# Scaling the rows of x by their gate ahead of the transposes, in four tiles of a routed expert layer

## The chip, the cores and the metric

One core of a Trainium2 chip runs the kernel. The metric is device time in microseconds (us): the median of several executions. The profile and the trace show one further execution; its times count from the start of its span. Engines are called as the profile calls them: PE is TensorE (PEld its weight loads), DVE is VectorE, ACT is ScalarE, POOL is GpSimd, SP is SyncE, which here only issues transfers.

## The reference

```python
def reference(**kwargs):
    attn_out = _attn_ref(**attn_kwargs)          # (4, 8, 544, 64)
    x = attn_out.transpose(0, 2, 1, 3).reshape(B * S, H * D)   # 2176 rows of 512
    x = _moe_ref(x=x, **moe_kwargs)
    return _moe2_ref(x=x, **moe2_kwargs)

def _moe_ref(x, w_gate, w1, w2, capacity):
    probs = softmax(x @ w_gate)                  # 8 experts
    expert_idx = np.argmax(logits, axis=1)
    gate_w = probs[np.arange(N), expert_idx]
    ...
    h = np.maximum(np.einsum('ecd,edf->ecf', disp, w1), 0.0)
    y = np.einsum('ecf,efd->ecd', h, w2)
    out[i] = gate_w[i] * y[expert_idx[i], pos[i]]

def _moe2_ref(x, w_in, w_out):
    h = x @ w_in
    g = h * np.clip(h + 3.0, 0.0, 6.0) / 6.0
    return g @ w_out
```

A row goes to one expert. Its gate is a positive number, and the expert is linear but for a ReLU, so that gate times expert(x) and expert(gate times x) are the same up to rounding.

## The kernel before

Three phases follow each other. The first computes the attention, the routing and the lists of rows of each expert, and one tile of the expert layer. The second, the loop of this case (`for s in range(N0, NF)`, s from 1 to 5), runs five tiles of 256 rows through their experts; "loop tile s" is one of them. The third multiplies all rows by the two last weight matrices, 16 slices of the inner size one after the other; its first group, of two row tiles, still converts the 64-bit words of these matrices to float (`vconv`, three DVE operations a piece, L1147, L1149, L1151), and `advance` spreads this conversion over the loop and that group.

The order of the work on each engine is that of the code: every engine takes its instructions in program order, and a wait holds all that stand behind it. One loop tile does this, in this order:

- `m1` (matmuls L904): four quarters q of the hidden layer, `xT` times W1, 24 matmuls each, in an exact split into high and low parts. Each quarter is taken out of PSUM by ACT (`ht` high part, `hth`, L908) and then by DVE (low part, `htl`, L910).
- After quarter 0 (`after0`): where the tile begins a new expert, the split of W2 (`split`, L825 on ACT, L827 with three pieces on DVE and one on POOL); then the gate row: PE transposes the 256 gates, broadcast to 128 columns, into PSUM (`row_turn`, L890, names `pgb`), and ACT copies them to `gB` (L894). After quarter 1 (`after1`): one `vconv` on DVE.
- `xt` (L847, `pxt`): PE transposes the gathered rows `xg` of the next tile, eight transposes; ACT and DVE take out high and low part (L850, L852).
- In tiles 2 and 4 transposes of a second stream, the half tiles (`p_...`), and in tiles 1 and 3 the split of W1 for the next expert.
- `m2` (L922): two halves of 48 matmuls. After the first half is taken out (`y_part`, L932: DVE multiplies PSUM, which holds y transposed, by the gate row and writes `y`), `between` computes the gate of the next tile (`gate`, L865 to L879: seven small DVE operations and one exponential on ACT). `y_out` sends y to DRAM.

`pm` in the rows stands for the PSUM tiles of `m1` and `m2`; four of them are in turn. The lines that matter for the gate:

```python
        hT = m1(xT.pop(s), {0: after0, 1: after1})
        ...
            xT[s + 1] = xt(xg[s + 1])
        ...
        m2(hT, ids.pop(s), gBs.pop(s), slice(256 * s, 256 * s + 256), between)
```

## Time and profile before

| | |
|---|---|
| median of 3 runs | 544.25 us (543.48 to 544.5) |
| the profiled execution | 542.06 us, of it 540.3 us span |
| granted TensorE clock, mean | 0.997 |
| PE busy | 524.3 us (97%) |
| DVE busy | 300.8 us (56%) |
| ACT busy | 219.1 us (41%) |
| POOL busy | 141.3 us (26%) |
| loop tiles 1 to 5 on PE | about 88 to 230.6 us |
| the third phase | from 230.6 us to the end |

The busy share of PE is of modelled ends of pipelined matmuls, so 97% does not say that PE never waits; where it waits is read from the idle time in the timeline of one engine. The timelines of one engine give start, duration, the operation, and in brackets the idle time ahead of it and what ended it. The profiled execution is 2.19 us below the median of the runs shown.

### The profile page before, as it was taken

The page shows a single profiled execution, that of the slowest core. Times are in us where ns is not written, and L with a number is a line of the kernel's source. Part 1 is how long each engine was busy: PE and PEld are TensorE (multiplying, and loading weights), DVE is VectorE, ACT ScalarE, POOL GpSimd, SP SyncE. Part 2 cuts the span into 40 slices and gives each one's busy share as a digit, 9 for nine tenths or more (in the row PEclk, how much of TensorE's full clock was granted, in tenths as well). Part 3 has the DMA queues.
Part 4 walks back from the last instruction along what each step waited for, and adds up shares of the span by engine and source line. Part 5 has one row for each costly group of instructions (what it writes and reads, how often), then busy time and mean ns, then how long its engine had stood idle before and what let it go on. Part 6 is the DMA issues. An engine that isn't in the chain of part 4 may idle for free.

```text
span 540.3 us, 10109 instructions
## 1 busy us (share of the span) xinstructions
PE 524.3 (97%) x3772; PEld 461.4 (85%) x3772; DVE 300.8 (56%) x722; ACT 219.1 (41%) x465; POOL 141.3 (26%) x201
## 2 busy tenths in 40 slices
PE   5999899999999999999999999999999999999995
PEld 3666899969789798999999889999999999888884
DVE  5889895359535763776989853343334344322332
ACT  4888752246024412344433442343233343332332
POOL 2657555016101100136767711001001000100002
PEclk9999999999999999999999999999999999999998
DMA  6855626979898965338653411011001010100002
GB/s 135 187 179 177 249 113 214 374 276 321 319 373 303 333 250 168 104 131 290 220 173 118 138 39 59 2 38 42 1 20 60 1 30 2 40 1 1 0 2 71
DMA packets 52169, 74.99 MB, mean 139 GB/s; under 512 B 23089, under 2 KB 31537, under 8 KB 51602
## 3 DMA queue, kind: packets, MB, share of 16 engines
q1 hardware_dynamic: 49362, 66.30, 36.4%
q0 software_dynamic: 2208, 7.38, 4.0%
q8 instruction: 32, 0.52, 0.4%
q10 hardware_dynamic: 544, 0.59, 0.3%
q14 instruction: 23, 0.19, 0.1%
HBM read 70.62 MB, written 16.23 MB: 161 GB/s over the span
## 4 chain that ended last, share of the span: by engine, by line
PE 52%; issue 25%; DMA 9%; DVE 5%; SPq 4%; POOL 3%; ACT 2%; POOLq 0%; ACTq 0%; DVEq 0%
PE p L1329 12%; PE po L1367 11%; PE pm L904 9%; PE pm L922 8%; PE pss L904 2%; DMA st<-in_moe_w_out_dram 2%; DMA raw<-in_moe_w_dram 2%; PE pm L1295 2%; PE pss L922 2%; SPq L815 1%; DVE v L1151 1%; SPq L101 1%; DMA y_pad<-xb 1%; DMA xb<-x_rows,ecol 1%; DMA st<-in_moe_w_in_dram 1%
## 5 line engine op out<-in xcount | busy, mean ns | idle before, releaser
L1329 PE MATMUL p<-yT,wh 128*128 128x256 f32 (+1 forms) x768 | 116.7, 294 | 0.0
L1329 PEld LDWEIGHTS p<-yT,wh 128*128 128x128 f32 x768 | 109.2, 188 | 7.8
L1342 DVE SCALAR_TENSOR_TENSOR g<-u,p 128x256 f32<-128x256 f32 x110 | 45.0, 409 | 107.6 <-ACT u L1341 106.0
L1341 ACT ACTIVATE u<-p,b 128x256 f32<-128x256 f32 x110 | 51.2, 465 | 102.6 <-PE p L1329 102.6
L1343 ACT CAST gh<-g 128x256 fp32r<-128x256 f32 x110 | 43.9, 399 | 79.5 <-DVE g L1342 79.0
L1524 POOL DMA_INDIRECT out_dram<-o,fid x14 | 13.6, 974 | 211.6 <-ACT o L1523 208.5
L1329 PE MATMUL p<-yT,wl 128*128 128x256 f32 (+1 forms) x384 | 66.7, 296 | 0.2 <-POOL wl L1166 0.2
L1367 PE MATMUL po<-wh,gh 128*128 128x512 f32 x156 | 61.2, 392 | 0.0
L1367 PE MATMUL po<-wh,gl 128*128 128x512 f32 x156 | 61.1, 392 | 0.0
L1367 PE MATMUL po<-wl,gh 128*128 128x512 f32 x156 | 61.0, 391 | 0.0
L904 PE MATMUL pm<-xt,w1h 128*128 128x256 f32 x320 | 57.5, 282 | 0.2 <-DVE lg L865 0.2
L1329 PEld LDWEIGHTS p<-yT,wl 128*128 128x128 f32 x384 | 55.4, 189 | 1.7 <-POOL wl L1166 0.6
L904 PEld LDWEIGHTS pm<-xt,w1h 128*128 128x128 f32 x320 | 48.7, 188 | 3.2 <-issue 3.1
L1349 DVE TENSOR_TENSOR gl<-g,gh 128x256 fp32r<-128x256 f32 x84 | 33.5, 399 | 32.2 <-ACT gh L1343 32.2
L922 PE MATMUL pm<-htl,w2h 128*128 128x256 f32 x160 | 44.8, 280 | 0.4 <-DVE htl L910 0.4
L922 PE MATMUL pm<-hth,w2h 128*128 128x256 f32 x160 | 45.0, 281 | 0.0
L922 PE MATMUL pm<-hth,w2l 128*128 128x256 f32 x160 | 44.6, 279 | 0.0
L904 PE MATMUL pm<-xt,w1l 128*128 128x256 f32 x160 | 44.0, 279 | 0.0
L1166 POOL TENSOR_TENSOR wl<-v,wh 128x1024 fp32r<-128x1024 f32 x13 | 32.3, 2484 | 35.0 <-DVE yT L1090 33.5
L1367 PEld LDWEIGHTS po<-wh,gl 128*128 128x128 f32 x156 | 29.3, 188 | 7.0 <-POOL gl L1349 0.4
L1349 POOL TENSOR_TENSOR gl<-g,gh 128x256 fp32r<-128x256 f32 x26 | 25.0, 961 | 30.3 <-ACT gh L1343 30.3
L1367 PEld LDWEIGHTS po<-wl,gh 128*128 128x128 f32 x156 | 29.3, 188 | 3.9
(316 smaller groups left out, 949.4 us busy)
## 6 DMA issues: line engine op xcount, KB each, us to landing
raw<-in_moe_w_dram SPq DMA_DIRECT2D x80, 512.0 KB
st<-in_moe_w_in_dram SPq DMA_DIRECT2D x16, 512.0 KB
st<-in_moe_w_out_dram SPq DMA_DIRECT2D x16, 512.0 KB
x_rows<-xrow SPq DMA_DIRECT2D x4, 1072.0 KB
xb<-in_x_dram SPq DMA_DIRECT2D x32, 128.0 KB
yg<-y_pad SPq DMA_DIRECT2D x13, 258.0 KB
out_dram<-zt SPq DMA_DIRECT2D x2, 1536.0 KB
y_pad<-y SPq DMA_DIRECT2D x5, 516.0 KB
```

Of the source, the lines that this page charges most:

```text
L101: nc.sync.dma_start(out=xbs[b][:, h // 2, :, h % 2, :], in_=x[b, h].rearrange("(p j) d -> p j d", j=4))
L904: T.matmul(ps[:, j], W1[l][k][:, ls], xT[r][:, k], start=n == 0, stop=n == 11)
L922: T.matmul(ps[:, j], W2[l][k // 2][:, k % 2, ls], hT[k // 2][r][:, k % 2], start=k == 0 and i == 0, stop=k == 7 and i == 2)
L1166: (V if m in (0, 2, 15) else G).tensor_tensor(out=wl, in0=v, in1=wh.bitcast(F32), op=ALU.subtract)
L1295: T.matmul(ps[s:s + m, :], th[:, a:a + m], raws[k // 2, g][:, 512 * (k % 2) + 256 * n:512 * (k % 2) + 256 * n + w], start=k == 0, stop=k == 7)
L1329: T.matmul(out, w[:, 128 * k:128 * k + 128], r(k), start=n == 0, stop=n == 11)
L1341: A.activation(out=u, in_=ps, func=AF.Relu, bias=b3)
L1342: V.scalar_tensor_tensor(out=g, in0=u, scalar=6.0, in1=ps, op0=ALU.min, op1=ALU.mult)
L1343: A.copy(gh[:, 0:w], g)
L1349: eng.tensor_tensor(out=gl, in0=g[:, 0:n], in1=gh[:, 0:n].bitcast(F32), op=ALU.subtract)
L1367: T.matmul(po[t], l[:, ls], r[:, 512:1024], start=m == 0 and i == 0, stop=m == 15 and i == 2)
L1524: G.indirect_dma_start(out=outs.pop() if outs else out, out_offset=bass.IndirectOffsetOnAxis(ap=fid[0:n, t:t + 1], axis=0), in_=o[0:n], in ...
```

## The change

For loop tiles 2 to 5 the gate is computed earlier, in `after1` of the tile before (a new function `gated`), and two DVE operations multiply the gathered rows in place, 128 rows by 512 numbers each (L1438). The transposed y then needs no gate: ACT copies it out of PSUM (L1227) where DVE multiplied. The gate rows of these tiles are not made. Loop tile 1 stays as it was.

```diff
@@ def m2 @@
             ps = pair_bank("pm2")
             m2_into(ps, hT, q)
-            y_part(y, ps, q, gB)
+            if gB is None:
+                A.copy(y[:, :, 256 * q:256 * q + 256].rearrange("p t (k j) -> p k t j", k=2), ps.rearrange("p k (t j) -> p k t j", t=2))
+            else:
+                y_part(y, ps, q, gB)
@@
+    def gated(s):
+
+        ids[s], gv = gate(xg[s])
+        for t in range(2):
+            v = xg[s][:, t].rearrange("p (f c) -> p f c", f=2)[:, :, 0:256]
+            V.tensor_scalar(out=v, in0=v, scalar1=gv[:, t:t + 1], scalar2=None, op0=ALU.mult)
+
@@ def after0 @@
-            gBs[s] = row(gvs.pop(s))
+            if s == N0:
+                gBs[s] = row(gvs.pop(s))
@@ def after1 @@
+            if not last:
+                gated(s + 1)
             if last:
@@ def between @@
-            if not last:
-                ids[s + 1], gvs[s + 1] = gate(xg.pop(s + 1))
@@
-            xT[s + 1] = xt(xg[s + 1])
+            xT[s + 1] = xt(xg.pop(s + 1))
@@
-        m2(hT, ids.pop(s), gBs.pop(s), slice(256 * s, 256 * s + 256), between)
+        m2(hT, ids.pop(s), gBs.pop(s, None), slice(256 * s, 256 * s + 256), between)
```

VectorE in loop tile 2, from the split of W2 to the low parts of the next tile's x; before:

```order
L827 TENSOR_TENSOR w2l_108<-raw,w2h_104 128x1024
L827 TENSOR_TENSOR w2l_110<-raw,w2h_106 128x1024
L827 TENSOR_TENSOR w2l_111<-raw,w2h_107 128x1024
L1447 UNCONDITIONAL_BRANCH x2
L910 SCALAR_TENSOR_TENSOR htl_2262<-pm_2263,hth_2261 128x512
L1147 TENSOR_SCALAR v_2171<-st 128x512
L1149 SCALAR_TENSOR_TENSOR v_2171<-st,v_2171 128x512
L1151 SCALAR_TENSOR_TENSOR v_2171<-st,v_2171 128x512
L910 SCALAR_TENSOR_TENSOR htl_2296<-pm_2297,hth_2295 128x512
L910 SCALAR_TENSOR_TENSOR htl_2325<-pm_2326,hth_2324 128x512
L852 TENSOR_TENSOR xt<-pxt,xt 128x4x128 x2
```

The same place in the changed kernel, from the low part of quarter 1 on:

```order
L910 SCALAR_TENSOR_TENSOR htl_2259<-pm_2260,hth_2258 128x512
L865 TENSOR_TENSOR lg<-xg 128x16
L867 TENSOR_REDUCE mx<-lg 128x2
L869 TENSOR_TENSOR lg<-lg,mx 128x16
L873 COPY idt<-xg 128x2
L875 TENSOR_REDUCE mx<-lg 128x2
L877 TENSOR_SCALAR mx<-mx 128x2
L879 RECIPROCAL mx<-mx 128x2
L1438 TENSOR_SCALAR xg<-xg,mx 128x2x256 x2
L1147 TENSOR_SCALAR v_2173<-st 128x512
L1149 SCALAR_TENSOR_TENSOR v_2173<-st,v_2173 128x512
L1151 SCALAR_TENSOR_TENSOR v_2173<-st,v_2173 128x512
```

The gate of tile 3 and its two multiplications now stand between the low part of quarter 1 and the conversion; the low parts of quarters 2 and 3 follow behind all of them.

ScalarE in loop tile 3, from the split of W2 on, as the difference (L871 is the exponential of the gate):

```order
-L894 COPY gB<-pgb 128x256
-L908 ACTIVATE hth_2718<-pm_2720 128x512
-L908 ACTIVATE hth_2753<-pm_2755 128x512
-L908 ACTIVATE hth_2782<-pm_2784 128x512
+L908 ACTIVATE hth_2712<-pm_2714 128x512
+L871 ACTIVATE lg<-lg 128x16
+L908 ACTIVATE hth_2760<-pm_2762 128x512
+L908 ACTIVATE hth_2789<-pm_2791 128x512
```

The copy of the gate row is gone, and the exponential now stands ahead of the high parts of quarters 2 and 3.

## Rows read from the trace of the kernel before

**Rows 1.** The page, part 1: busy time, share of span, instructions.

```profile
PE 524.3 (97%) x3772; PEld 461.4 (85%) x3772; DVE 300.8 (56%) x722; ACT 219.1 (41%) x465; POOL 141.3 (26%) x201
```

**Rows 2.** The chain in order of time: start us, us, what.

```profile
248.11 5.66 DMA st<-in_moe_w_out_dram
...
269.02 6.26 DMA st<-in_moe_w_in_dram
```

**Rows 3.** Windows: length; PE, PEld, DVE, ACT, POOL busy; granted clock; DMA share; GB/s.

```profile
230.60:244.40 13.80, 13.80 (x98) 12.79 (x98) 10.87 (x21) 6.32 (x14) 5.62 (x5) 1.00 0.35 116
```

**Rows 4.** Timeline of DVE, around loop tile 2.

```profile
118.63 0.16 DVE L865 TENSOR_TENSOR lg<-xg 128x16 f32<-128x16 f32 x1
...
119.89 0.17 DVE L879 RECIPROCAL mx<-mx 128x2 f32<-128x2 f32 x1
119.97 0.15 DVE L865 TENSOR_TENSOR lg<-xg 128x8 f32<-128x8 f32 x1
...
125.50 0.68 DVE L910 SCALAR_TENSOR_TENSOR htl<-pm,hth 128x512 fp32r<-128x512 f32 x1
126.09 2.93 DVE L827 TENSOR_TENSOR w2l<-raw,w2h 128x1024 fp32r<-128x1024 f32 x1
...
131.22 0.68 DVE L910 SCALAR_TENSOR_TENSOR htl<-pm,hth 128x512 fp32r<-128x512 f32 x1
131.82 0.41 DVE L1147 TENSOR_SCALAR v<-st 128x512 int32<-128x512 int32 x1
...
133.61 1.28 DVE L910 SCALAR_TENSOR_TENSOR htl<-pm,hth 128x512 fp32r<-128x512 f32 x2
```

**Rows 5.** Timeline of POOL, loop tile 2.

```profile
125.53 2.42 POOL L827 TENSOR_TENSOR w2l<-raw,w2h 128x1024 fp32r<-128x1024 f32 x1 [8.50 <-ACT w2h L825]
...
131.38 1.00 POOL L859 DMA_INDIRECT xg<-x_rows,col  x1 [0.30 <-issue]
```

**Rows 6.** Timeline of PE, loop tile 2.

```profile
121.75 0.38 PE L890 MATMUL pgb<-identk,mx 128*128 128x128 f32 x2
...
130.57 1.04 PE L847 MATMUL pxt<-identk,xg 128*128 128x128 f32 x8
...
132.24 0.36 PE L922 MATMUL pm<-hth,w2h 128*128 128x256 f32 x1
...
134.34 0.38 PE L922 MATMUL pm<-htl,w2h 128*128 128x256 f32 x1 [0.38 <-DVE htl L910]
```

**Rows 7.** Timeline of ACT, loop tiles 2 and 4.

```profile
126.91 0.60 ACT L908 ACTIVATE hth<-pm 128x512 fp32r<-128x512 f32 x1
...
199.41 0.21 ACT L871 ACTIVATE lg<-lg 128x16 f32<-128x16 f32 x1 [5.92 <-DVE idt L873]
```

**Rows 8.** Timelines of POOL and then DVE, in the third phase.

```profile
265.39 1.18 POOL L1349 TENSOR_TENSOR gl<-g,gh 128x256 fp32r<-128x256 f32 x1
...
265.90 0.96 DVE L1147 TENSOR_SCALAR v<-st 128x512 int32<-128x512 int32 x1
```

**Rows 9.** Timelines of POOL, DVE and PE, in this order, loop tile 4.

```profile
186.03 2.69 POOL L827 TENSOR_TENSOR w2l<-raw,w2h 128x1024 fp32r<-128x1024 f32 x1 [12.97 <-ACT w2h L825]
...
190.32 0.41 DVE L1147 TENSOR_SCALAR v<-st 128x512 int32<-128x512 int32 x1
...
190.96 1.03 PE L847 MATMUL pxt<-identk,xg 128*128 128x128 f32 x8
...
192.19 0.36 PE L922 MATMUL pm<-hth,w2h 128*128 128x256 f32 x1
```

**Rows 10.** Timelines of DVE and PE, loop tiles 1 and then 3.

```profile
95.32 0.42 DVE L1147 TENSOR_SCALAR v<-st 128x512 int32<-128x512 int32 x1
...
99.28 1.04 PE L847 MATMUL pxt<-identk,xg 128*128 128x128 f32 x8
...
158.88 0.42 DVE L1147 TENSOR_SCALAR v<-st 128x512 int32<-128x512 int32 x1
...
163.04 1.04 PE L847 MATMUL pxt<-identk,xg 128*128 128x128 f32 x8
```

## The prediction

> **What bounds the kernel now.** The page's busy line comes first [rows 1]: PE is busy 97% of the span and no other engine is above 56%, so time is won or lost where PE waits. The timeline of PE then shows where that is in the loop. There is one wait of weight in loop tile 2: the fourteenth matmul of m2 starts at 134.34, held by a low part (`htl`) from DVE [rows 6]. The thirteen matmuls before it run from 132.24 at about 0.114 us each, so without the wait it would have started at about 133.7: 0.65 us are lost there. [...] Behind 244 us the chain of waits runs over DVE conversions and the loads they free (three such loads, 5.5 to 6.3 us each, first and last in [rows 2]); that too is paced by PE's arrival, so I shift it as one piece.

> DVE is the engine to read next, since both things that PE would wait for come from it. In loop tile 2 it is a queue without gaps of weight from 118.6 to 134.9 [rows 4].

> **The change part by part.**

> *Gate rows.* Eight transposes leave PE, two in each of four tiles. A pair is busy 0.38 us [rows 6], overlapped with its neighbours; between nothing and 0.38 us I take 0.2 us a pair, the middle. In tiles 3 and 5, where nothing else holds PE, that is a gain of 0.4 us. In tiles 2 and 4 the next wait swallows it (below). The four copies of the row leave ACT, which hides them before.

> *The exit of y.* Eight multiplications out of PSUM leave DVE, of the size of its other 128x512 operations from PSUM, 0.68 us [rows 4], some 5.4 us in all; eight copies come to ACT, where an operation of that size from PSUM takes 0.60 us [rows 7]. ACT idles 5.92 us ahead of the gate's exponential in m2 of tile 4 [rows 7], so the copies are covered; if they were not, a PSUM tile would come free up to 0.6 us later, of which four are in turn. The relief of DVE lies in m2, where PE does not wait for it. I cost both at nothing.

> *The gate moves, with two multiplications, ahead of the transposes.* This is the term that decides. PE takes `pxt` straight after m1; in the changed order it must wait there for the gate and the multiplications of the next tile, which DVE reaches only after the low part of quarter 1, and that stands behind the split of W2 wherever a new expert begins: in tiles 2 and 4. PE's queue holds behind that wait the half tiles' transposes and all of m2. The gate takes, from its first operation at 118.63 to the end of its last at 119.89 + 0.17, 1.43 us with ACT's exponential inside [rows 4]; add 0.03 for the hand-over. The multiplication (128x512, SBUF to SBUF, one source, a scalar per partition) is not in the trace. Nearest is the first conversion step, one source and 128x512, 0.41 us [rows 4]; the same step took 0.96 us where POOL was at work [rows 8]. I take 0.41, as nearest in form, and 0.35 for the start-to-end step of the second one behind it; 0.96 stays for the range.
> [...]

> *Tile 2.* The gate of tile 2 no longer stands in tile 1's m2, so the gate of the half tile starts at 118.63 and not at 119.97 [rows 4], and all behind it comes 1.34 us earlier: the low part of quarter 0 at 124.16, the split at 124.75. One piece of the split alone takes 1.2 us (2.93 + two more end as the next low part starts at 131.22 [rows 4]), so the first ends at 125.98. POOL's piece is ready at 125.53 [rows 5]. Before, DVE's first piece came second and was held until POOL was through (125.53 + 2.42 = 127.95, and 1.07 us later it ended, at 129.02). Now POOL is held by DVE, and as one waiting gets its turn when the other's instruction ends (POOL's `gl` was issued at 265.39 under a running DVE operation, and DVE's next one, issued at 265.90, was the one that then took 0.96 and not 0.41 us [rows 8]), POOL works from 125.98 to about 128.3, DVE's second piece ends at 129.35, the third at 130.5. ACT had all its casts done before 126.91 [rows 7], so it does not hold this. Low part of quarter 1 to 131.1, its successor starting 0.08 us before that; gate from 131.0, multiplications 132.47 to 132.88 and 133.2. PE's transposes, at 130.57 before [rows 6], start at about 132.95: 2.4 us later. The old wait of 0.65 us for the low part of quarter 2 goes: it is ready at 133.2 + 1.8 (one conversion) + 0.7 = 135.7, and its matmul comes at 133.7 + 2.4 = 136.1. Net 2.4 - 0.65, about **1.8 us later**.

> *Tile 4.* Here the split's last DVE piece ends when POOL lets go, as before (186.03 + 2.69 = 188.72, and 1.07 us), so nothing comes earlier. The slot that the conversion has at 190.32 [rows 9] goes to the gate: multiplications from 190.32 + 1.46 = 191.78 to 192.19 and 192.55. The transposes, at 190.96 before [rows 9], start at 192.3: **1.35 us later**. The low part of quarter 2 is ready at 192.55 + 1.8 + 0.7 = 195.05; its matmul, 13 after the start of m2 at 192.19 + 1.35, comes at 195.1. That just fits.

> *Tiles 1 and 3.* No split stands ahead of the gate. It starts at 95.32 and 158.88, ends with its multiplications 2.25 us later (97.6 and 161.15), and the transposes come at 99.28 and 163.04 [rows 10]: covered by 1.7 and 1.9 us.

> *ACT's order.* The exponential now stands ahead of the high parts of quarters 2 and 3. In tile 2 it waits for DVE until 131.2, so these high parts come at 131.4 and 132.0 where the first stood at 128.0; DVE asks for them only after the conversion, at 135.0. Hidden, by 2.4 us. SP and POOL issue the same transfers; some loads are freed 1.3 us earlier.

> **Sum.** 1.8 + 1.35 - 0.4 = 2.75 us later. Against the profiled execution, 542.06 us: 544.8. That execution stands 2.2 us below the median of the runs; on their scale 544.25 + 2.75 = **547.0 us**, 0.5% slower. About 0.2% is what a measurement of this kernel can tell from no change.

> **Rivals.**
> - *DVE keeps its turn in tile 2.* If DVE's three pieces run back to back ahead of POOL's, they end at 128.3 instead of 130.5; POOL then works until 130.65, the multiplications slip in at 130.65 to 131.35, PE starts 0.5 us late and loses no more than the old wait. Tile 2 costs nothing, the sum is 1.35 - 0.4 = 0.95: 545.2, which counts as the same. For: one of the two must yield. Against: [rows 8]. Chance 0.11.
> - *The multiplications are held by POOL.* In tile 2 POOL issues gathers from 128 to 134. If a multiplication had to wait out one gather (1.00 us [rows 5]), tile 2 costs 1 us more: 548.0. Against: the conversion step at 131.82 ran in 0.41 us inside such a gather [rows 4, 5]. [...] Chance 0.13.
> - *On the other side: the multiplications are covered.* If DVE, relieved of 5.4 us, came to the gate early enough, all four gate rows (0.8) and the old wait (0.65) are won: 542.8. It decides at 130.6 in tile 2 and 190.9 in tile 4: the second multiplication would have to end there. For: DVE is ahead by 1.34 us in tile 2. Against: in tile 4 the split ends with POOL's piece, which no relief of DVE moves. Chance 0.06.
> - *The delay is absorbed behind 244 us.* If the loads of [rows 2] were in fact ahead of PE, a later PE would find them done, and 2 to 3 of some 17 us of waiting would go: 544 to 544.5. Against: each is issued when a conversion frees its buffer, and these follow PE's pace. Chance 0.08.

> **How the numbers follow.** The forecast has 0.62; its own range is 546.6 to 549.0, the upper end with 0.96 us for each multiplication, about 1 us more in either tile. The range reaches down to the first rival, with half a microsecond for the runs: 544.6 to 549.0; it leaves out the last two rivals (0.14) and little else. Slower: 0.62, 0.13 and 0.03 of the first rival, 0.78. Same: the rest of that rival and most of the absorbed case, 0.14. Faster: 0.08.

> **What would show it.** In the changed trace PE should stand idle ahead of `pxt` in tiles 2 and 4, about 2.4 and 1.35 us, released by DVE's L1438, and not in tiles 1 and 3; the wait ahead of the low part of quarter 2 should be gone or below 0.2 us; L1438 should last about 0.41 us; from the loop's end to the end of the span the length should be as before within 0.5 us. The prediction falls if L1438 runs ahead of PE in tile 2, if the pieces of the split swap the other way, or if the third phase is shorter by what the loop is longer.

## The result, and the profile after

| | before | changed |
|---|---|---|
| median of 7 runs, us | 543.48 (542.04 to 544.5) | 547.59 (545.48 to 551.05) |
| ratio, 95% interval | | 1.0091 [1.0067, 1.0115] |
| profiled execution, its span, us | 542.06, 540.3 | 551.05, 549.1 |

The change makes the kernel slower by 0.7 to 1.2%, some 4.1 us. The forecast was 547.0 in 544.6 to 549.0, and 2.75 us more than before. Side and range hold; the loss is half as large again as the working said, and the rest of this text is about that half. The profiled execution of the changed kernel is the slowest of its seven.

The busy line of the changed kernel, against [rows 1]:

```profile
PE 527.7 (96%) x3764; PEld 464.1 (85%) x3764; DVE 298.5 (54%) x722; ACT 223.0 (41%) x469; POOL 141.7 (26%) x201
```

PE has eight instructions fewer and is busy 3.4 us longer. Work did not grow, so either PE was slower for a while or it was waiting in a way that counts as busy. Its timeline in loop tiles 2 and then 4, against [rows 6, 9]:

```profile
133.67 0.28 PE L904 MATMUL pm<-xt,w1l 128*128 128x256 f32 x1
136.94 1.89 PE L847 MATMUL pxt<-identk,xg 128*128 128x128 f32 x8 [2.99 <-issue]
138.62 1.91 PE L1284 MATMUL pht<-identk,h 128*128 128x128 f32 x8
140.19 0.50 PE L922 MATMUL pm<-hth,w2h 128*128 128x256 f32 x1
...
199.64 1.09 PE L847 MATMUL pxt<-identk,xg 128*128 128x128 f32 x8 [1.81 <-DVE xg L1438]
200.86 0.66 PE L1284 MATMUL pht<-identk,h 128*128 128x128 f32 x4
```

The waits stand where they were forecast: ahead of `pxt`, in tiles 2 and 4. The first one is put down to "issue"; that it is the same wait is read from DVE. The first of its two multiplications (L1438, here 0.72 us) ends at 136.89, just ahead of the transposes at 136.94:

```profile
129.45 1.22 DVE L827 TENSOR_TENSOR w2l<-raw,w2h 128x1024 fp32r<-128x1024 f32 x1
131.83 2.18 DVE L827 TENSOR_TENSOR w2l<-raw,w2h 128x1024 fp32r<-128x1024 f32 x1 [1.16 <-ACT w2h L825]
133.93 0.68 DVE L910 SCALAR_TENSOR_TENSOR htl<-pm,hth 128x512 fp32r<-128x512 f32 x1
134.53 0.16 DVE L865 TENSOR_TENSOR lg<-xg 128x16 f32<-128x16 f32 x1
...
136.17 1.11 DVE L1438 TENSOR_SCALAR xg<-xg,mx 128x512 f32<-128x512 f32 x2
137.20 0.41 DVE L1147 TENSOR_SCALAR v<-st 128x512 int32<-128x512 int32 x1
```

This is the queue that the prediction drew: split of W2, low part of quarter 1, gate, multiplications. But what stands *behind* the wait is new. The eight transposes took 1.04 us before [rows 6]; now the two groups of eight take 1.89 and 1.91. The windows of PE say why: the wait, then the transposes, then m2 (columns as in [rows 3]).

```profile
133.90:136.90 3.00, 0.05 (x1) 0.00 (x0) 2.63 (x11) 1.19 (x3) 2.42 (x4) 1.00 1.05 384
136.90:140.20 3.30, 3.26 (x17) 3.26 (x17) 3.23 (x7) 1.65 (x3) 2.65 (x5) 0.53 1.05 386
140.20:151.70 11.50, 11.50 (x98) 11.37 (x96) 3.41 (x8) 1.28 (x3) 2.42 (x3) 0.99 0.78 292
```

Behind 2.99 us without work the granted clock was 0.53 for 3.3 us. At that rate 3.3 us hold 1.55 us less work, as an estimate from this window: 3.30 x (1 - 0.53). In tile 4 the wait of 1.81 us was followed by a clock of 1.00:

```profile
199.60:201.50 1.90, 1.74 (x14) 1.50 (x15) 1.83 (x4) 1.07 (x2) 0.00 (x0) 1.00 1.04 384
```

The rest of the document uses one table. A **stage** is read from starts in PE's timeline: tile 2 from the first matmul of its m1 to the first of the half tile's second product (`p_m2`) behind its m2; each later stage begins where the one before ends, at the end of m2, and tile 5 ends with the third phase's first matmul. The stretch is the sum of tiles 2 to 5.

| profiled execution | tile 2 | tile 3 | tile 4 | tile 5 | stretch |
|---|---|---|---|---|---|
| before | 25.10 | 31.81 | 27.91 | 26.74 | 111.56 |
| changed | 29.31 | 31.40 | 29.56 | 26.54 | 116.81 |
| difference | +4.21 | -0.41 | +1.65 | -0.20 | +5.25 |

From the end of that stretch to the end of the span both kernels need the same: the third phase's first matmul starts at 230.41 of 540.3 before and 239.21 of 549.1 now, which leaves 309.9 us in each.

```profile
239.21 1.10 PE L1332 MATMUL p<-yT,wh 128*128 128x256 f32 x8
```

So nothing of the loop's delay is taken up later. The profiled spans differ by 8.8 us, more than these 5.25: m1 of tile 2 already starts 3.55 us later, at 122.40 and not 118.85. About 1.7 us of that, as an estimate from the next window, 3.50 x (1 - 0.51), is the clock too, in the first phase, whose code is the same in both kernels (PE stood 1.41 us for gathered rows until 60.2 us, and 1.7 us after that the clock fell):

```profile
61.90:65.40 3.50, 3.50 (x18) 3.50 (x18) 3.50 (x20) 3.33 (x7) 1.84 (x4) 0.51 0.08 18
```

The experiment that follows repeats the changed kernel without that fall, and the kernel before had a wait of 1.42 us in that place with the clock at 1.00 behind it. Another 1.16 us lie in tile 1, where PE stood 1.02 us just ahead of tile 2, against 0.18 us before, for DVE, whose split of W1 came late (its last piece ended at 121.65, and at 118.10 before); in the repeat tile 1 is 0.07 us longer than before. Both are left out of the change's account.

### The profile page after: what moved, and what is told of

Same layout as the page of the kernel before. It is cut to its first block, busy times and chain, and to the rows that moved or that the text cites. A ratio compares the mean times of both kernels' runs of the same rounds, so it can differ in the third digit from the quotient of the medians.

```text
span 549.1 us, 10106 instructions
## 1 busy us (share of the span) xinstructions
PE 527.7 (96%) x3764; PEld 464.1 (85%) x3764; DVE 298.5 (54%) x722; ACT 223.0 (41%) x469; POOL 141.7 (26%) x201
## 4 chain that ended last, share of the span: by engine, by line
issue 41%; PE 38%; DMA 8%; DVE 5%; POOL 3%; ACT 3%; SPq 2%; POOLq 0%; ACTq 0%; DVEq 0%
PE pm L922 8%; PE pm L904 7%; PE p L1332 5%; PE po L1370 4%; DMA raw<-in_moe_w_dram 3%; PE pss L904 2%; PE pss L922 2%; PE pm L1298 2%; POOL out_dram L1535 2%; PE psx L277 2%; DMA st<-in_moe_w_in_dram 1%; PE pss L285 1%; DMA xb<-x_rows,ecol 1%; SPq L815 1%; DVE v L1149 1%
## 6 DMA issues: line engine op xcount, KB each, us to landing
xb<-in_x_dram SPq DMA_DIRECT2D x32, 128.0 KB
```

## The experiments

The theory: PE waits for L1438 in tiles 2 and 4 as forecast, and what the forecast lacks is the clock behind the longer of the two waits. The rivals: the waits alone are longer than forecast (no clock in it); the moved gate costs by its place, whatever it multiplies; the copies on ACT or the relieved exit of y have a price of their own. Medians below are of 6 to 12 runs, against 23 to 29 runs of the kernel before on the same chip, 541.9 to 542.2 us.

**e_again: the changed kernel once more, unedited.**

> The changed kernel once more, for a second profile. Measure: the stretch from the first matmul of m1 in loop tile 2 to the first matmul of the third phase, 111.7 us in the kernel before (118.85 to 230.57) and 117.0 in the first profile of the changed one (122.40 to 239.37). Theory (PE waits for the multiplications in tiles 2 and 4, and after the longer of the two waits the granted clock falls for some us): 114.5 us if the clock holds at 1.00 behind the wait of tile 2, 116 to 117 if it falls again to about half. Rival (the extra in tile 2 was the W2 load that landed late in that one execution, at 130.7): 114.5 whatever the clock does, and the load of this profile lands earlier against the start of the tile.

(The expectation takes the end of the stretch 0.16 us later than the table does, in both kernels.) 546.65 us, ratio 1.0086 [1.0061, 1.0111]. Tile 2 is +3.91, tile 4 +1.82, the stretch 116.79, within 0.02 us of the first profile. The wait in tile 2 is shorter, the clock falls again:

```profile
134.25 1.59 PE L847 MATMUL pxt<-identk,xg 128*128 128x128 f32 x8 [2.67 <-DVE xg L1438]
135.65 1.91 PE L1284 MATMUL pht<-identk,h 128*128 128x128 f32 x8
```

The window of the transposes:

```profile
134.20:137.20 3.00, 2.95 (x16) 2.95 (x17) 2.93 (x6) 1.63 (x3) 2.60 (x5) 0.58 1.04 383
```

The wait that PE shows is here put down to L1438. In tile 4 it is 1.80 us, and the eight transposes behind it take 1.09 us, as in the first profile, where the clock was 1.00. The rival of the late load of W2 falls but for a small part. DVE stood 1.16 us ahead of the last piece of the split in the first profile, and 0.27 us here:

```profile
128.24 3.08 DVE L827 TENSOR_TENSOR w2l<-raw,w2h 128x1024 fp32r<-128x1024 f32 x1 [0.27 <-ACT w2h L825]
```

So the transposes come 14.24 us after the start of m1 and not 14.54. Behind their start both profiles need the same 14.77 us to the end of the stage.

**e_24 and e_35: the change for half of the tiles.** `gated(s + 1)`, run in m1 of tile s, is named by the tile whose x it multiplies. e_24 keeps it for tiles 2 and 4, so that it runs in m1 of tiles 1 and 3; e_35 keeps it for 3 and 5, so that it runs in m1 of 2 and 4, behind the split of W2. The other two tiles keep the gate in `between` and its row.

```diff
-            if not last:
+            if not last and s + 1 in (2, 4):    # e_35: (3, 5)
                 gated(s + 1)
...
```

> Only loop tiles 2 and 4 have their rows multiplied (prepared in tiles 1 and 3, where no split of W2 stands ahead of the gate); tiles 3 and 5 keep gate row and multiplied y. Theory: no wait ahead of the transposes, stretch of the loop 110.5 to 111.5 us, time as before within 0.2%, or 0.1 to 0.2% less. Rival (the loss comes from y leaving by ACT, or from the gate's exponential ahead of the high parts): half of the change's edits are here, so half of its loss, a stretch of about 114 us and 0.4% slower.

> Only loop tiles 3 and 5 have their rows multiplied (prepared in tiles 2 and 4, behind the split of W2); tiles 2 and 4 keep gate row and multiplied y. Theory: the whole loss is here: waits ahead of the transposes of 2.5 to 4.5 us in tile 2 (the gate of tile 2 still stands in tile 1's m2, so DVE comes 1.3 us later than in the changed kernel) and about 2 us in tile 4, stretch 116 to 118.5 us, 0.8 to 1.2% slower. Rival (y by ACT): a stretch of about 114 us, as with tiles 2 and 4.

e_24: 540.61 us, 0.9967 [0.9952, 0.9983]: faster than before, and the lowest median measured. Stages: -0.26, -0.20, -0.67, +0.01, together 110.44. Of tile 4's gain 0.64 us lie in m1; a gate row accounts for some 0.2 of that, and for the rest the matmuls there start 0.113 us apart and not 0.118 as before (the changed kernel's first profile has 0.113 there too, at a clock of 1.00, and the kernel before has its 0.118 at 1.00). What sets that spacing was not tried. The transposes of tile 2 follow m1 without a wait:

```profile
129.53 0.28 PE L904 MATMUL pm<-xt,w1l 128*128 128x256 f32 x1
129.65 1.03 PE L847 MATMUL pxt<-identk,xg 128*128 128x128 f32 x8
130.53 1.04 PE L1284 MATMUL pht<-identk,h 128*128 128x128 f32 x8
```

e_35: 548.53 us, 1.0112 [1.0084, 1.0139], with all of the loss: tile 2 +5.57, tile 4 +1.30, the stretch 117.98.

```profile
133.75 1.97 PE L847 MATMUL pxt<-identk,xg 128*128 128x128 f32 x8 [3.38 <-DVE xg L1438]
```

Windows of the transposes, of the first part of m2 and of the rest of it:

```profile
133.70:137.10 3.40, 3.35 (x17) 3.35 (x17) 3.33 (x7) 1.66 (x3) 0.54 (x1) 0.50 1.05 393
137.10:139.50 2.40, 2.40 (x13) 2.40 (x12) 1.21 (x3) 0.68 (x2) 0.82 (x2) 0.51 1.04 392
139.50:149.20 9.70, 9.70 (x87) 9.62 (x85) 2.41 (x4) 0.00 (x0) 1.37 (x2) 1.00 0.72 256
```

The same edit wins where no split of W2 stands ahead of the gate and loses where one does. Behind the longest wait, 3.38 us, the clock stayed low the longest, 5.8 us at 0.50 and 0.51, 2.4 us of them in m2. That the copies of y on ACT cost something by themselves falls: e_24 has half of them and is faster.

**e_gate and e_gate2: the gate's place alone.** The kernel before, with only its gate moved from `between` to `after1`; no multiplication of x, rows made as before. The second is the first once more.

```diff
         def after1():
+            if not last:
+                ids[s + 1], gvs[s + 1] = gate(xg[s + 1])
...
         def between():
-            if not last:
-                ids[s + 1], gvs[s + 1] = gate(xg.pop(s + 1))
...
```

> The kernel before with only the gate moved into the place that the change gives it (behind the low part of quarter 1, the exponential ahead of the high part of quarter 2); no multiplication of rows, gate rows and multiplied y as before. The transposes then have nothing to wait for. Theory: no idle time ahead of the transposes, a stretch of 111 to 112 us, time as before. Rival (the place of the gate on DVE and ACT is itself what costs, by late low parts): 113 us or more.

> The run with the gate alone moved, once more: it was 0.33% slower (0.18 to 0.48), but in its profile the loop itself was only 0.3 us longer than before once a fall of the clock at the start of tile 2 (behind a wait of 2.3 us for late W1 weights) is taken out. Theory (the place of the gate costs 0.5 us in tile 4, where the low part of quarter 2 comes late, and nothing in tile 2; the rest was that wait, which is not of the edit): 0.05 to 0.2% slower, stretch 111.5 to 112.2 us where the clock holds. Rival (the place of the gate costs 1.5 us or more by itself): 0.3% slower again and a stretch of 113 us with the clock at 1.00.

e_gate: 543.82 us, 1.0033 [1.0018, 1.0048]. In its profile PE stood 2.33 us for DVE at the start of tile 2, with a clock of 0.57 behind it, which hides what the gate does; hence the second run.

```profile
122.65 0.36 PE L904 MATMUL pm<-xt,w1h 128*128 128x256 f32 x1 [2.33 <-DVE lg L865]
...
122.60:126.60 4.00, 3.95 (x20) 3.98 (x21) 3.60 (x12) 1.18 (x3) 0.00 (x0) 0.57 0.73 260
```

e_gate2: 543.83 us, 1.0031 [1.0012, 1.0050], stretch 113.01, with the clock at 1.00 at that start. Its expectation was missed: the gate's place does cost, 1.45 us in the stretch, tile 2 +0.96 and tile 4 +0.48. PE waits for the low part of quarter 2, which the gate has pushed back on DVE:

```profile
137.85 0.39 PE L922 MATMUL pm<-htl,w2h 128*128 128x256 f32 x1 [1.15 <-DVE htl L910]
...
198.04 0.38 PE L922 MATMUL pm<-htl,w2h 128*128 128x256 f32 x1 [0.31 <-DVE htl L910]
```

This is the wait that the kernel before has in tile 2 as well [rows 6], made longer. It is no part of the changed kernel's loss to be added on top: there PE comes to this matmul late, because of `pxt`, and finds the low part done. One late DVE queue shows at one place or the other.

**e_early: the same gates and multiplications, but a tile earlier.** The gate of tile s + 2 and its multiplications are put at the end of m2 of tile s; that of tile 2 stays in m1 of tile 1.

```diff
         def after1():
-            if not last:
+            if s == N0:
                 gated(s + 1)
...
+        if s + 2 < NF:
+            gated(s + 2)
         steps(1 if s > N0 else 2)
```

> All four tiles multiplied, but the gate and the multiplications of tiles 3 to 5 stand one place earlier, at the end of m2 of the tile before the one that transposes them, so ahead of the split and not behind it. Theory: no wait for the multiplications at any transpose; in tile 2 DVE's queue is about 1 us longer than before, which comes out at the low part of quarter 2: stretch 111.5 to 113 us, time within 0.2% of before. Rival (y by ACT, or anything else in the edits but the place of the gate): the loss stays, 115 to 117 us.

543.02 us, 1.0012 [0.9993, 1.0031]: no difference from before that can be told. All four tiles are multiplied ahead of their transposes, none waits there, tile 4 is -0.23. Tile 2 is +1.51, by the old place again:

```profile
132.68 0.39 PE L922 MATMUL pm<-htl,w2h 128*128 128x256 f32 x1 [0.17 <-DVE htl L910]
...
135.06 0.38 PE L922 MATMUL pm<-htl,w2h 128*128 128x256 f32 x1 [1.41 <-DVE htl L910]
```

So the loss of the change belongs to the place of the multiplications in DVE's queue, not to the multiplications.

**e_fill: the changed kernel with PE kept at work.** 22 matmuls in tile 2 and 14 in tile 4, on data at hand and into a bank whose values nobody reads, stand ahead of the transposes. They take away PE's idleness and leave the wait.

```diff
+            if p is not None:
+                fill = p3.tile([128, 512], F32, name="pxt", tag="3")
+                for i in range(FILL[s]):
+                    T.matmul(fill[:, 0:256], W1[0][i % 4][:, 0:128], xs[0][:, i % 4], start=True, stop=True)
             xT[s + 1] = xt(xg.pop(s + 1))
...
```

> The changed kernel, with idle matmuls put where PE waits: 22 in loop tile 2 and 14 in tile 4, of the shape of those of m1, into a PSUM tile that nobody reads, straight ahead of the transposes. Both waits for the multiplications stay. Theory (the granted clock falls because PE stands idle in tile 2, and this is a part of the loss of its own): the clock stays at 1.00, the eight transposes and the eight behind them take 0.9 and 0.8 us instead of 1.4 to 1.9 and 1.6, and the stretch of the loop falls from 116.8 to 115.0 to 115.6 us, 0.2 to 0.3% under the changed kernel. Rival (the transposes are slow behind the wait because DVE, or a late load, feeds them slowly): the stretch stays at 116.8 or grows by what the idle matmuls overrun.

545.93 us, 1.0074 [1.0056, 1.0092]. In the profile (its lines are one further down) PE works through, and the transposes run at a granted clock of 1.00. They start 14.05 us after m1, against 14.24 and 14.54 in the two profiles of the changed kernel, so that the filling does not hold them up:

```profile
129.97 2.75 PE L1498 MATMUL pxt<-xt,w1h 128*128 128x256 f32 x22
132.61 1.09 PE L848 MATMUL pxt<-identk,xg 128*128 128x128 f32 x8
133.84 1.09 PE L1285 MATMUL pht<-identk,h 128*128 128x128 f32 x8
```

The window of the transposes:

```profile
132.60:134.70 2.10, 1.96 (x19) 1.72 (x17) 2.03 (x5) 1.23 (x3) 1.72 (x4) 1.00 1.07 397
```

Tile 2 is +2.43 instead of +3.91 and +4.21. Not all of the 1.5 to 1.8 us between them is the clock's: the transposes come 0.2 to 0.5 us sooner here. From their start to the end of the stage it is 13.48 us here and 14.77 in both of those: 1.29 us are the clock's, somewhat less than the 1.55 us estimated above. Tile 4, where the clock had not fallen, is +1.58 instead of +1.65 and +1.82: the filling gives it next to nothing. The stretch, 114.96, is at the lower edge of what was expected; the time is not in it. It is only 0.7 us (0.13%) under e_again, where 0.2 to 0.3% was expected, and the two intervals overlap: the stages show the clock's share, the medians alone do not.

**e_late, e_early_late, e_24_late: one conversion out of DVE's way.** The conversion step that `after1` puts behind quarter 1 goes behind quarter 3, in the kernel before, in e_early and in e_24.

```diff
         def after1():
...
-            steps(1)
+            if last:
+                steps(1)
+
+        def after3():
+            if not last:
+                steps(1)
...
```

> The kernel before with only the conversion of quarter 1 put behind quarter 3. Theory: its one wait of the loop (0.65 us at the low part of quarter 2 in tile 2) goes, nothing else: stretch 110.8 to 111.1 us, 0.1% faster, hardly to be told from the kernel before; so what the run of all four edits wins beyond that is the gate rows. Rival: no difference in the stretch.

> All four tiles multiplied, the gate and multiplications one place earlier (as in the run with them at the end of m2, stretch 112.2 us), and the conversion that stood behind quarter 1 put behind quarter 3, so that the low part of quarter 2 need not wait for it. Theory: the 1.4 us of waiting for that low part in tile 2 go, and nothing else is late: stretch 110 to 110.8 us, about 0.3% faster than the kernel before. Rival (the conversions are late for the third phase then, or the low parts wait for POOL and not for DVE's queue): 112 us, or a third phase longer than 309.7 us.

> Rows multiplied for tiles 2 and 4 only, and the conversion of quarter 1 put behind quarter 3. Theory: the two gains add as far as they are of different waits (the gate rows and the shorter queue of DVE in the first, the low part of quarter 2 of tile 2 in the second, of which the first has already won most): stretch 109.9 to 110.4 us, 0.3 to 0.4% faster than the kernel before. Rival: they are the same gain, stretch 110.4 us as with the first edit alone.

e_late: 541.36 us, 0.9988 [0.9973, 1.0004], stretch 110.84; tile 2 is -0.72, so the old wait of 0.65 us is gone. e_early_late: 541.02 us, 0.9979 [0.9966, 0.9992], stretch 110.12; its wait of 1.41 us is gone and only this one is left:

```profile
133.39 0.38 PE L922 MATMUL pm<-htl,w2h 128*128 128x256 f32 x1 [0.18 <-DVE htl L910]
```

e_24_late: 541.22 us, 0.9983 [0.9969, 0.9996]. Its stretch is the shortest, 109.62, below the 109.9 to 110.4 expected, but the gain in time, 0.17% (0.04 to 0.31), lies below the 0.3 to 0.4% expected and cannot be told from that of e_24. A microsecond in the loop is at the edge of what the runs can tell.

## Why the prediction was right or wrong

*PE waits ahead of `pxt` in tiles 2 and 4 and not in 1 and 3*: right; e_24 and e_35 show it on the two halves.

*Tile 2, 1.8 us.* This is the term that failed. It measured 3.9 to 4.2. The working took 2.4 us of wait less the old wait of 0.65, and priced the wait as lost time and no more. The wait first. The low part of quarter 1 starts 11.53 us after m1 (122.40 to 133.93) where the working had about 11.55, but by another way: two pieces of the split, not one, ran ahead of POOL's on DVE, so that the rival in which DVE keeps its turn was half right, and the last piece was held by ACT's cast, which waited 0.83 us for a load of W2 (1.16 us of idle DVE), and then by POOL: it took 2.18 us and ended 1.08 us behind POOL's piece, where the two ahead took 2.35 us together.

```profile
129.99 2.94 POOL L827 TENSOR_TENSOR w2l<-raw,w2h 128x1024 fp32r<-128x1024 f32 x1 [9.42 <-ACT w2h L825]
```

That the time agrees is luck; in e_again, with the load earlier, it is 11.24. Behind it the gate takes 1.64 us and not 1.46, and the first multiplication 0.72 and not 0.41. So the transposes come 2.5 to 2.8 us later than before and not 2.4, and PE's idle time is 2.67 and 2.99.

What stands behind the wait is the larger part. From the start of the transposes the stage should have been 0.65 us shorter than before; it is 1.4 us longer (14.77 against 13.38). 1.29 us of that are the term that is missing from the sum: the granted clock behind the wait. The page of the kernel before had hidden it, since the longest idle time of PE in its loop is 0.38 us [rows 6]. The other 0.75 us stand in e_fill too, where the clock held. Some 0.35 of them lie between the two groups of transposes, which start 1.23 us apart in e_fill and 0.88 before; the register load and the branch of PE's own program that stand there are shown under tile 4. Some 0.3 lie in m2, of whose matmuls about half start 0.116 to 0.121 us apart and not 0.113. e_24 and e_fill have the same share of these without a wait or a fall, so they are not the clock's; what sets the spacing was not tried.

*Tile 4, 1.35 us*: 1.65 and 1.82. The mechanism is right, and so is the place of the transposes: they start 12.95 us after m1 in both profiles, 1.32 later than before. (PE's idle time is longer, 1.81, because m1 had become 0.6 us shorter, by the gate row and by the spacing of its matmuls.) What the working lacks is 0.4 us behind them. The half tiles' transposes start 1.22 us after the first of `pxt` (199.64 to 200.86) and not 0.87 as before:

```profile
191.83 0.60 PE L1281 MATMUL pht<-identk,h 128*128 128x128 f32 x4
```

Between the two PE's own sequencer (PEldq in the rows) takes a register load (0.30 us) and a branch (0.35 us). The kernel before did that under the matmuls of m1 (0.30 and 0.22 us); now it comes behind the wait, and the branch (200.45 to 200.80) ends 0.06 us ahead of the half tiles' transposes. Its rows, before and now:

```profile
L1488 PEldq COMPARE_BRANCH  x1: 224/224/224, 190.2 to 190.2; - x1
L1499 PEldq COMPARE_BRANCH  x1: 352/352/352, 200.4 to 200.4; - x1
```

In the kernel before, where PE had no wait, the branch ends 1.4 us ahead of these transposes. They start 1.21 us after the first of `pxt` in e_again, 1.15 in e_fill and 1.08 in e_35, and 0.87 to 0.88 in e_24 and e_early, where PE had no wait.

*L1438 in 0.41 us, taken from the conversion step*: short.

```profile
L1438 DVE TENSOR_SCALAR xg<-xg,mx x8: 468/484/717, 99.2 to 199.5; 128x512 f32<-128x512 f32 x8
...
  PEld pxt L847: 2.0, 1
  PE pxt L847: 1.8, 1
```

The median is 0.48 us and the longest 0.72, in no case the 0.96 of the upper bound.

*The gate rows, -0.4 us in tiles 3 and 5*: -0.41 and -0.20, together -0.6. But not all of that is the rows: e_35, which leaves out the rows of tiles 3 and 5 alone, has -0.23 and -0.22, and e_24, which keeps them, -0.20 and +0.01. So a pair is worth 0.2 us, the middle that was taken, and the rest in tile 3 comes with the other half of the change.

*The old wait for the low part of quarter 2 goes*: right, no such wait stands in the changed timeline.

*The exit of y, at nothing*: right. The copies on ACT took 0.587 us, PE's waits in the loop are the two ahead of `pxt` and the 1.02 us ahead of tile 2, none of them for a PSUM bank, and e_24, which has them, is faster.

```profile
L1227 ACT COPY y<-pm x8: 579/587/588, 146.2 to 239.4; 128x512 f32<-128x512 f32 x8
```

*From the loop's end to the end of the span as before*: right, 309.9 us in both, so that the loop's delay is handed on whole. With that the rival of an absorbed delay falls. Covered multiplications fall with the waits above, and so does a tile 2 that costs nothing because DVE keeps its turn. Multiplications held by POOL: at most 0.3 us of one (0.72 us the longest, 0.47 the shortest), not a whole gather of 1.00 us.

By terms the sum would have been 4.21 + 1.65 - 0.61 = 5.25 us, and the two profiles of the changed kernel both show that. The runs' medians show 4.1 and 4.7. They spread with the mean granted clock: of the seven runs, the two with 0.998 took 545.48 and 546.24 us, and the one with 0.992 took 551.05. Part of that spread is the first phase's clock, so it is not the change's alone. Nor need the clock fall behind the wait in every run: of the 13 runs of the changed kernel, five have a mean clock of 0.997 or 0.998, as all six of e_fill have, and their median, 546.24 us, is near e_fill's 545.93. No trace of these five is kept, so this is not shown. And that the forecast of 547.0 came so near to 547.59 is in part luck: the runs of the kernel before had come out 0.77 us lower than those it was added to.

## What to carry to other kernels

A wait of PE, which bounds this kernel, cost its length and, where the clock fell behind it, part of the work behind it again: waits of 2.67 and 2.99 us, with clocks of 0.58 and 0.53 behind them, cost 1.3 us on top, against e_fill. Steps of PE's own program that had run under queued work, a register load of 0.30 us and a branch of 0.35, showed behind the wait of tile 4 as well, by some 0.35 us. So a step that delays PE was worth pricing with more than the wait. Moving work earlier in the program was worth nothing where it landed behind a block that was itself late: the same edit gained 0.3% in the tiles where the queue ahead was short (e_24, in part by the spacing of matmuls, which is not explained) and lost 1.1% where a weight split stood in it (e_35).

## What had not been expected of the hardware

At a clock of 1.00 the matmuls of m1 and m2 start mostly 0.113 or 0.118 us apart in the kernel before (0.118 in m1 of tile 2, 0.113 in its m2). In m1 of tile 4 nearly all went from 0.118 in the kernel before to 0.113 in the changed one, which is 0.4 us of its 96 matmuls. The two profiles of the gate moved alone differ so in m1 of tile 2 (0.113 in e_gate, from 128.5 us on, 0.118 in e_gate2), so it is not the order of the code alone. No run was made to find what sets it.

The multiplication by a scalar per partition, in place and on two blocks of 256 in each row, took 0.47 to 0.72 us, against 0.41 for the conversion's integer step of the same 128x512. Whether the layout, the type or the scalar makes the difference was not tried either.
